# An early one-kilobyte load, the place of its transpose, and new due times in a planned attention and feed-forward kernel

## The chip, the cores and the metric

The kernel runs on one core of a Trainium2 chip. A core has five engines with a queue of instructions each: PE (TensorE, matrix products; its weight loads are listed as PEld), DVE (VectorE), ACT (ScalarE), POOL (GpSimd) and SP (SyncE, which issues most transfers). Sixteen DMA engines move data between the device memory and the core's memory. Engines wait for one another through semaphores. The metric is device microseconds (us) of one execution, the median of several runs; smaller is better.

## The reference

Two blocks read the same x (2048 rows of 512, bf16) and are mixed by a gate per row:

```python
def _A_ref(x, wqkv, wo):                       # H = 32 heads of 16, window W = 256
    q, k, v = qkv[0], qkv[1], qkv[2]           # from x @ wqkv
    scores = jnp.einsum("bhqd,bhkd->bhqk", q, k) * (Dh ** -0.5)
    mask = (idx[:, None] - idx[None, :] >= 0) & (idx[:, None] - idx[None, :] < W)
    scores = jnp.where(mask[None, None], scores, -1e9)
    p = _softmax(scores, axis=-1)
    o = jnp.einsum("bhqk,bhkd->bhqd", p, v)
    return (...)(o, 0, 2, 1, 3).reshape(B, S, D) @ wo

def _B_ref(x, w1, w3, w2):                     # F = 1376
    h = _silu(x @ w1) * (x @ w3)
    return h @ w2

g = _sigmoid((x * gate_w).sum(-1, keepdims=True))
return g * _A_ref(x, A_wqkv, A_wo) + (1 - g) * _B_ref(x, B_w1, B_w3, B_w2)
```

The einsums of the feed-forward block are written here as products.

## The kernel before

**What PE has to do.** The rows are taken in 16 tiles of 128 and 4 quarters of 512 (index `tq` or `tcb`). Attention goes through four columns `c` of 128 features (eight heads each). For a column and a quarter `projections` computes k, q (L374, four matmuls of 512 columns each) and v (L432). For each of the 16 row tiles, `main_batch` computes scores into the tile `su` (L493, eight matmuls), ScalarE takes their exponential into `E` (L498), VectorE masks the diagonal (L479), and `pv` multiplies with v (L588). Every quarter also has a `far_batch` (L525 and, in the last, L533) for the far edge of the window; GpSimd masks that (L552). `pv` divides by the sum and multiplies by the gate on VectorE (L596, L599), and SP transposes the result into `OT` by a DMA (L605).

The feed-forward block works quarter by quarter: 11 blocks `f` of up to 128 features with w1 and w3 (L651, four matmuls of 512 columns for each of the two), tanh on ScalarE (L656), two VectorE operations (L660, L665) into `hT`, and then the product with w2 for four row tiles (L702). `output` multiplies `OT` with wo (L731), adds the feed-forward part (L735) and stores (L740).

The partial results of all these products go through four banks of PSUM, `ch`; the scores have a place of their own, `su`.

**What sets the order.** Nothing is scheduled by the compiler. `opening` (L255) writes its instructions in the order of the code: zeros for `warm`, the identity, 27 matmuls of zeros (`warm_up`, L253), then all the loads. A load on `nc.sync` is issued by SP, one on `nc.scalar` by ScalarE's queue. `load_w` (L245) loads a weight block for a range of features; with `both=True` SP takes its first half and ScalarE's queue the second. In the built program the DMAs take eight semaphores in turn, and a DMA that takes one again waits until the earlier transfer of that semaphore has landed.

All later work is a list of operations in a `Plan`. Each has an engine, an expected duration, what it depends on, the buffers it takes and frees, and a due time. `emit` (L62) walks through an imagined time: of the operations that can start first, it writes the one with the earliest due time. The imagined landing times of the loads are the table `landed`. So due times and `landed` set the order in which instructions stand in each engine's queue; the hardware then works through each queue in that order. The due times come from four numbers: attention is spread evenly over `TA` from `T0` (`at(c, t)`), the feed-forward block from `TF0` to `TF1` (`ffn_due`). Projections are due a `lead` before the scores they serve, P·V and the outputs some us after `at`.

**The opening.** x's first quarter is loaded plainly and turned on PE (L312, 16 transposes of 128 columns), then evacuated (L317 on VectorE, L319 on ScalarE). Then come eight more zeros (`warm_up(8)`, L328). The first feed-forward block f = 0 is cut in halves of 256 columns, so that it can begin when half of the quarter is there. gate_w, 512 numbers, is loaded as four rows of 128 (`gwr`) and turned on PE by a tiny transpose (`gw_turn`, L334); VectorE copies the result next to the first 128 columns of wv (L338, L342), so that the v projection of column 0 gives the gate's sum as a 129th column. In the program before, PE's instructions stand thus: 27 zeros, 16 transposes of x, 8 zeros, w1 for the first half, the turn of gate_w, w3 for the first half, w1 for the second half, k, q, w3 for the second half, w1 of f = 1, v, the first scores, w3 of f = 1.

Of the kernel before, what the change touches and what calls it, by code (L numbers as in the profile page):

```python
# [15 lines left out]
P = 128  # L16
# [22 lines left out]
class Plan:  # L39
# [6 lines left out]
    def add(self, eng, dur, fn, deps=(), due=0.0, take=(), free=(), lat=None):  # L46
        if lat is None:
            lat = 0.2 if eng == "PE" else 0.08
        op = Op(eng, dur, fn, deps, due, list(take), list(free), lat, len(self.ops))
        self.ops.append(op)  # L50
        return op
# [73 lines left out]
def kernel(  # L125
# [20 lines left out]
    NDC = D // P  # L146
# [21 lines left out]
    w3_sb = pp.tile([P, NDC, F], BF16, name="w3_sb")  # L168
# [24 lines left out]
    ch = [ps.tile([P, 512], F32, name=f"ch_{i}") for i in range(4)]  # L193
# [3 lines left out]
    add = plan.add  # L197
# [47 lines left out]
    def load_w(dst, src, f0, f1, both=False):  # L245

        rows = src[:, f0:f1].rearrange("(c p) f -> p c f", p=P)
        for eng, c0, c1 in ((nc.sync, 0, 2), (nc.scalar, 2, 4)) if both else ((nc.sync, 0, 4),):
            eng.dma_start(out=dst[:, c0:c1, f0:f1], in_=rows[:, c0:c1, :])

    def warm_up(n):
        for i in range(n):
            nc.tensor.matmul(su[:, 0, 0:P], lhsT=warm[:], rhs=warm[:], start=True, stop=True)  # L253

    def opening():  # L255
        nc.vector.memset(warm[:], 0.0)
        constants()
        warm_up(WARM)

        nc.scalar.activation(out=gt[:, 0:4], in_=warm[:, 0:4], func=ACT.Tanh)  # L260
        load_x(0, 2, nc.sync)
        load_x(2, 4, nc.scalar)
        load_w(w1_sb, B_w1, 0, 2 * P, True)
        load_w(w3_sb, B_w3, 0, 2 * P, True)
        nc.scalar.dma_start(out=gwr[:], in_=gate_w.rearrange("(c p) -> c p", p=P))
        for b in (1, 0, 2):
            load_w(wqkv_sb, A_wqkv, b * D, b * D + 2 * P)
        for f0, f1, tq in ((2 * P, 6 * P, 1), (6 * P, F, 2)):
            load_w(w1_sb, B_w1, f0, f1)
            load_w(w3_sb, B_w3, f0, f1)  # L270
            turn_x(tq)
        nc.sync.dma_start(out=w2_sb[:, 0:NFC - 1, :],
                          in_=B_w2[0:(NFC - 1) * P, :].rearrange("(f p) n -> p f n", p=P))
        nc.sync.dma_start(out=w2_sb[0:FL, NFC - 1, :], in_=B_w2[(NFC - 1) * P:F, :])
        turn_x(3)
        nc.sync.dma_start(out=wo_sb[:], in_=A_wo.rearrange("(c p) n -> p c n", p=P))
        for b in (1, 0, 2):
            load_w(wqkv_sb, A_wqkv, b * D + 2 * P, (b + 1) * D)
        constants2()
        constants3()  # L280
        constants4()
        constants5()


    T0, TA, TF0, TF1 = 10.0, 234.0, 4.0, 246.0
    step = TA / (NDC * NT)
    landed = {"x": [4.0, 4.1, 15.6, 22.0, 30.0], "w13": [4.9, 5.6, 12.6, 19.8], "w2": 28.5,
              "qkv": [6.6, 7.4, 8.2, 34.0], "wo": 31.5, "gw": 5.8}

    def at(c, t):  # L290
        return T0 + step * (c * NT + t)
# [4 lines left out]
    x_in = [arrive(u) for u in landed["x"]]  # L296
    w13_in = [arrive(u) for u in landed["w13"]]
    qkv_in = [arrive(u) for u in landed["qkv"]]
    gw_in = arrive(landed["gw"])
# [4 lines left out]
    for m in range(4):  # L304
# [16 lines left out]
        a = add("PE", 0.25, tr, [x_in[m // 2]], 0.1 * m, take=[(job, "ch")])  # L321
# [3 lines left out]
    for tq in range(1, NTC):  # L325
        xt_ready[tq].append(x_in[tq + 1])

    add("PE", 0.44, lambda: warm_up(8), [x_in[1]], 0.5)  # L328


    gjob = Job()
# [9 lines left out]
    def wv0_copy():  # L341
        nc.vector.tensor_copy(out=wv0[:, :, 0:P], in_=wqkv_sb[:, :, 2 * D:2 * D + P])  # L342

    a = add("PE", 0.1, gw_turn, [gw_in], 7.0, take=[(gjob, "ch")])
    wv0_ready = [add("DVE", 0.15, gw_out, [a], 9.0, free=[(gjob, "ch")]),
                 add("DVE", 0.3, wv0_copy, [qkv_in[2]], 9.0)]
    gate_ready = []
# [7 lines left out]
    ejob = {}  # L355

    def projections(c, tq):
        lead = 14.0 if c else 3.0
        due = at(c, 4 * tq) - lead
        war = []  # L360
        if c:
# [18 lines left out]
        a = plan.pieces(HALF, 0.2172, lambda lo, hi: chain(kj, D, lo, hi), src[:-1] + [qkv_in[0 if c < 2 else 3]], due, [(kj, "ch")])  # L380
# [23 lines left out]
            k_ready[(c, tq)] = [m0, m1]  # L404

        qj = Job()
        qdue = due if tq == 0 else at(c, 4 * tq - 4) - lead + 4.0

        qeng = "ACT" if (c, tq) == (0, 0) else "DVE"

# [3 lines left out]
        a = plan.pieces(HALF, 0.2172, lambda lo, hi: chain(qj, 0, lo, hi), src[:-1] + [qkv_in[1 if c < 2 else 3]] + qwar, qdue, [(qj, "ch")])  # L414
# [6 lines left out]
        for m0, nm in ([(4 * tq, 2), (4 * tq + 2, 2)] if c == 0 else [(4 * tq, 4)]):  # L421
# [26 lines left out]
            if c == 0:  # L448
                a = plan.pieces((0, 1, 2), 0.225, vmm, src + vwar + wv0_ready, vdue, [(vj, "ch")])
            else:  # L450
                a = plan.pieces(HALF, 0.225, vmm, src + vwar, vdue, [(vj, "ch")])
# [115 lines left out]
        return res, last_mask  # L567

    def pv(c, i, main, far):
        due = at(c, i) + 2.0  # L570
        job = Job()
        blocks = []
        for back in (2, 1, 0):
            if i - back >= 0:
                blocks.append((i - back, 0, P * back))
                blocks.append((i - back, 1, 320 + P * back))
        deps = [main[t] for t, par, off in blocks if par == 0]
        if i >= 2:
            deps.append(far[i - 2])
        for tq in sorted({t // 4 for t, par, off in blocks}):  # L580
            deps += v_ready[(c, tq)]

        def mm(lo, hi):
            po = ch[job.at["ch"]]
            for s in range(lo, hi):
                for bi, (t, par, off) in enumerate(blocks):
                    e = E[ejob[(c, t // 4)].at["E"]][:, t % 4, s].rearrange("p a q -> p (a q)")
                    nc.tensor.matmul(po[:, 34 * s:34 * s + 34], lhsT=e[:, off:off + P],  # L588
                                     rhs=vbd[:, 2 * t + par, s, :], start=(bi == 0),
                                     stop=(bi == len(blocks) - 1))  # L590

        def po8(job):
            return ch[job.at["ch"]][:, 0:8 * (DH + 1)].rearrange("p (h d) -> p h d", d=DH + 1)

        def rec():
            nc.vector.reciprocal(out=rden[job.at["oc"]][:], in_=po8(job)[:, :, DH:DH + 1])  # L596

        def norm():
            nc.vector.scalar_tensor_tensor(out=oc[job.at["oc"]][:], in0=po8(job)[:, :, 0:DH],  # L599
                                           scalar=gq[:, i:i + 1],  # L600
                                           in1=rden[job.at["oc"]][:].to_broadcast([P, 8, DH]),
                                           op0=ALU.mult, op1=ALU.mult)

        def tr():
            nc.sync.dma_start_transpose(out=OT[:, c, i * P:(i + 1) * P],  # L605
                                        in_=oc[job.at["oc"]][:].rearrange("p h d -> p (h d)"))

        frees = [(ejob[(c, h)], "E") for h in range(max(0, i - 2) // 4, i // 4 + 1)]
        a = plan.pieces(HALF, 0.026 * len(blocks), mm, deps, due, [(job, "ch")], free=frees)
        pv_ops[(c, i)] = a  # L610
        b = add("DVE", 0.21, rec, [a], due, take=[(job, "oc")])
        d = add("DVE", 0.35, norm, [b, gate_ready[i // 4]], due, free=[(job, "ch")])
        ot_ready[(c, i)] = add("SP", 1.1, tr, [d], due, free=[(job, "oc")], lat=1.3)
# [25 lines left out]
    for tcb in range(NTC):  # L639
        hj = Job()  # L640
        hs = []
        for f in range(NFC):
            fs = fsz(f)
            due = ffn_due(1.73)
# [24 lines left out]
            if tcb == 0 and f == 0:  # L669

                def half_first(j, w, k, half=half):
                    return lambda: half(j, w, 0, NDC, t0=256 * k, t1=256 * (k + 1))

                a = add("PE", 0.436, half_first(job, w1_sb, 0), xt_ready[0][0:2] + [w13_in[0]], due,
                        take=[(job, "ch")])
                b = add("PE", 0.436, half_first(up, w3_sb, 0), [a, w13_in[1]], due, take=[(up, "ch")])
                a = add("PE", 0.436, half_first(job, w1_sb, 1), xt_ready[0][2:4] + [a], due)
# [15 lines left out]
        for mm in range(4):  # L693
            m = 4 * tcb + mm
            due = ffn_due(2.38)
# [25 lines left out]


    def output(m, n0, n1, queue):
        due = at(NDC - 1, m) + 6.0
        job = Job()
        part = n1 - n0

        def omm(lo, hi):
            pso = ch[job.at["ch"]]
            for c in range(lo, hi):  # L730
                nc.tensor.matmul(pso[:, 0:part], lhsT=OT[:, c, m * P:(m + 1) * P], rhs=wo_sb[:, c, n0:n1],  # L731
                                 start=(c == 0), stop=(c == NDC - 1))

        def oev():
            nc.vector.tensor_tensor(out=ot[job.at["ot"]][:, 0:part], in0=ch[job.at["ch"]][:, 0:part],  # L735
                                    in1=bsb[:, m, n0:n1], op=ALU.add)

        def odma():
            eng = nc.sync if queue == "SP" else nc.scalar
            eng.dma_start(out=out2d[m * P:(m + 1) * P, n0:n1], in_=ot[job.at["ot"]][:, 0:part])  # L740

        a = plan.pieces(HALF, 0.2172 * part / 512, omm, [ot_ready[(c, m)] for c in range(NDC)] + [wo_in], due,
                        [(job, "ch")])
        b = add("DVE", 0.69 * part / 512 + 0.02, oev, [a, b_ready[m]], due, take=[(job, "ot")],
                free=[(job, "ch")])
        add(queue, 0.55, odma, [b], due, free=[(job, "ot")], lat=1.3)
# [39 lines left out]
```

## Time and profile before

| | |
|---|---|
| runs of the kernel | 256.56 us median (254.38, 256.56, 256.69) |
| profiled execution | 257.61 us |
| its span (first to last instruction) | 255.8 us |
| PE busy | 248.4 us |
| VectorE, ScalarE, GpSimd busy | 184.4, 183.2, 107.8 us |
| PE matmuls of w1 and w3 (L651) | 360, 89.9 us |
| scores' exponentials (L498) | 60, 1876 ns each |
| mean granted clock of PE | 0.993 |

The span begins with the first instruction that the profiler recorded and ends with the last; the time has some 1.8 us around it. Busy time of a group is the time in which at least one of its instructions was under way; matmuls overlap, so their mean duration is longer than the distance at which they follow one another. A digit of the clock's line is the clock that PE was granted, in tenths of full speed.

### The profile page before, as it was taken

Reading aid. Unit: us, or ns where it says so; the run is one execution under the profiler, and the core shown is the slowest. Engines: PE = TensorE matmul, PEld = TensorE weight load, DVE = VectorE, ACT = ScalarE, POOL = GpSimd, SP = SyncE. Lnnn points to the kernel's source line nnn. Section 1 sums busy time; section 2 is a strip of 40 time slices with the busy share of each in tenths; the row PEclk is TensorE's granted clock in tenths of the full one; section 3 lists DMA queues with packets and bytes.
Section 4 is the critical chain, followed back from the end, with each engine's and each line's share of the span. In section 5 each row is a group of like instructions: output and inputs, shape, how many; then the busy total and the mean of one; then the engine's idle time right before and its main releaser. Section 6 shows DMA issues by size and latency. Waiting matters only on the chain.

```text
span 255.8 us, 8017 instructions
## 1 busy us (share of the span) xinstructions
PE 248.4 (97%) x3440; PEld 135.2 (53%) x3440; DVE 184.4 (72%) x402; ACT 183.2 (72%) x181; POOL 107.8 (42%) x97
## 2 busy tenths in 40 slices
PE   8699999999999999999999999999999999999995
PEld 8354555655464555555464555555554545545462
DVE  5168789867478888776478878867578787787562
ACT  3077889888677888867678797976588677685521
POOL 7000946070346364592357464473165460290300
PEclk9799999999999999999999999999999999999999
DMA  7999920000000000000000000000010111111112
GB/s 205 303 256 246 274 64 10 14 8 13 10 8 18 13 12 8 14 14 13 5 13 13 11 12 14 14 5 18 3 23 26 33 49 32 52 30 51 49 33 67
DMA packets 28107, 13.14 MB, mean 51 GB/s; under 512 B 17352, under 2 KB 28072, under 8 KB 28072
## 3 DMA queue, kind: packets, MB, share of 16 engines
q1 hardware_dynamic: 27104, 12.04, 19.4%
q10 hardware_dynamic: 968, 0.59, 0.7%
q8 instruction: 27, 0.44, 0.7%
q14 instruction: 8, 0.07, 0.1%
HBM read 6.85 MB, written 2.10 MB: 35 GB/s over the span
## 4 chain that ended last, share of the span: by engine, by line
PE 91%; DMA 5%; ACT 1%; DVE 1%; issue 0%; SPq 0%; DVEq 0%
PE ch L651 30%; PE ch L702 15%; PE ch L588 14%; PE ch L374 11%; PE su L493 8%; PE ch L432 6%; PE ch L731 5%; PE su L525 2%; DMA OT<-oc 2%; DMA gwr<-in_gate_w_dram 2%; ACT E L498 1%; DMA w_sb<-in_B_w_dram 1%; DVE ot L735 0%; DVE vbd L442 0%; PE su L533 0%
## 5 line engine op out<-in xcount | busy, mean ns | idle before, releaser
L498 ACT ACTIVATE E<-su 128x2048 bf16<-128x2048 f32 x60 | 112.6, 1876 | 33.1 <-PE su L493 32.5
L552 POOL TENSOR_SCALAR_AFFINE_SELECT E<-E 64x1024 bf16<-64x1024 bf16 x56 | 65.5, 1169 | 80.1 <-ACT E L540 77.7
L651 PE MATMUL ch<-xT,w_sb 128*128 128x512 bf16 (+2 forms) x360 | 89.9, 378 | 0.0
L398 POOL TENSOR_SCALAR kbd<-kt,rowsA 128x512 bf16<-128x512 bf16 x24 | 37.5, 1572 | 51.9 <-DVE kt L395 34.3
L588 PEld LDWEIGHTS <-E 128*128 128x128 bf16 x1440 | 43.7, 96 | 12.5 <-issue 2.7
L651 PEld LDWEIGHTS <-w_sb 128*128 128x128 bf16 (+1 forms) x360 | 31.6, 100 | 30.9 <-issue 4.6
L588 PE MATMUL ch<-vbd,E 128*128 128x34 bf16 x1440 | 46.3, 177 | 0.1
L702 PE MATMUL ch<-w_sb,hT 128*128 128x512 bf16 (+1 forms) x176 | 43.7, 380 | 0.0
L479 DVE TENSOR_TENSOR E<-E,mdiag 128x512 bf16<-128x512 bf16 x64 | 34.1, 533 | 12.7 <-ACT E L498 11.8
L660 DVE SCALAR_TENSOR_TENSOR h<-tt,ch 128x512 bf16<-128x512 bf16 (+1 forms) x44 | 30.1, 684 | 8.5 <-ACT tt L656 7.9
L374 PE MATMUL ch<-xT,wqkv_sb 128*128 128x512 bf16 x128 | 35.3, 388 | 0.0
L540 ACT ACTIVATE E<-su 128x2048 bf16<-128x2048 f32 (+1 forms) x16 | 26.6, 1663 | 12.2 <-PE su L525 7.2
L656 ACT ACTIVATE tt<-ch 128x512 bf16<-128x512 f32 (+1 forms) x44 | 26.1, 594 | 10.2 <-PE ch L651 9.8
L665 DVE SCALAR_TENSOR_TENSOR hT<-h,ch 128x512 bf16<-128x512 bf16 (+1 forms) x44 | 30.2, 686 | 4.2 <-PE ch L651 0.4
L702 PEld LDWEIGHTS <-hT 128*128 128x128 bf16 (+1 forms) x176 | 15.2, 97 | 17.1 <-issue 2.1
L599 DVE SCALAR_TENSOR_TENSOR oc<-ch,gq,rden 128x128 bf16<-128x128 f32 x64 | 22.5, 351 | 2.3
L493 PE MATMUL su<-qT,kbd 32*128 32x256 bf16 x480 | 23.8, 273 | 0.0
L596 DVE RECIPROCAL rden<-ch 128x8 f32<-128x8 f32 x64 | 13.1, 204 | 12.8 <-PE ch L588 12.5
L493 PEld LDWEIGHTS <-kbd 32*128 32x128 bf16 x480 | 7.1, 92 | 23.4 <-issue 22.9
L707 DVE TENSOR_SCALAR bsb<-ch,omg 128x512 bf16<-128x512 f32 x15 | 11.2, 749 | 10.6 <-PE ch L702 10.4
L374 PEld LDWEIGHTS <-wqkv_sb 128*128 128x128 bf16 x128 | 11.1, 100 | 11.9 <-issue 3.0
L731 PE MATMUL ch<-wo_sb,OT 128*128 128x512 bf16 (+1 forms) x68 | 16.6, 366 | 0.6 <-DMA OT<-oc 0.6
(54 smaller groups left out, 146.5 us busy)
## 6 DMA issues: line engine op xcount, KB each, us to landing
out_dram<-ot SPq DMA_DIRECT2D x15, 128.0 KB, 1.8
wqkv_sb<-in_A_wqkv_dram SPq DMA_DIRECT2D x6, 256.0 KB, 5.5
w_sb<-in_B_w_dram SPq DMA_DIRECT2D x1, 1280.0 KB, 7.0
w_sb<-in_B_w_dram SPq DMA_DIRECT2D x2, 608.0 KB, 4.5
w_sb<-in_B_w_dram SPq DMA_DIRECT2D x2, 512.0 KB, 4.8
OT<-oc SPq DMA_TRANSPOSE x64, 2.2
wo_sb<-in_A_wo_dram SPq DMA_DIRECT2D x1, 512.0 KB, 5.0
xs<-in_A_x_dram SPq DMA_DIRECT2D x1, 256.0 KB, 2.9
```

What stands on the lines that cost most here:

```text
L374: nc.tensor.matmul(pst[:], lhsT=wqkv_sb[:, dc, col + c * P:col + (c + 1) * P], rhs=xT[:, dc, tq * 512:(tq + 1) * 512], start=(dc == 0), st ...
L398: nc.gpsimd.tensor_scalar_mul(out=kv[:, :, h, :], in0=kt[kj.at["kt"]][:].rearrange("p (k t) -> p k t", t=KB), scalar1=rowsA[:, h:h + 1])
L479: nc.vector.tensor_tensor(out=e, in0=e, in1=mdiag[:, None, :].to_broadcast([P, 8, KB]), op=ALU.min)
L493: nc.tensor.matmul(su[:, s, par * 256:(par + 1) * 256], lhsT=kbd[r, 2 * t + par, :, :].rearrange("p a k -> p (a k)"), rhs=qT[r, q0:q0 + 25 ...
L498: nc.scalar.activation(out=E[ej.at["E"]][:, t % 4, :, :, 0:256], in_=su[:].rearrange("p s (a q) -> p s a q", a=2), func=ACT.Exp, scale=SCALE)
L552: nc.gpsimd.affine_select(out=e[lo:lo + KB], in_=e[lo:lo + KB], pattern=[[0, 16], [-1, KB]], compare_op=ALU.is_ge, fill=0.0, base=-1, chan ...
L588: nc.tensor.matmul(po[:, 34 * s:34 * s + 34], lhsT=e[:, off:off + P], rhs=vbd[:, 2 * t + par, s, :], start=(bi == 0), stop=(bi == len(bloc ...
L651: nc.tensor.matmul(ch[job.at["ch"]][0:fs, t0:t1], lhsT=w[:, dc, f * P:f * P + fs], rhs=xT[:, dc, tcb * 512 + t0:tcb * 512 + t1], start=(dc ...
L660: nc.vector.scalar_tensor_tensor(out=h1[job.at["h1"]][0:fs, :], in0=tt[job.at["tt"]][0:fs, :], scalar=1.0, in1=ch[job.at["ch"]][0:fs, :], ...
L665: nc.vector.scalar_tensor_tensor(out=hT[0:fs, f, :], in0=h1[job.at["h1"]][0:fs, :], scalar=0.5, in1=ch[up.at["ch"]][0:fs, :], op0=ALU.mult ...
L702: nc.tensor.matmul(bps[:], lhsT=hT[0:fs, f, mm * P:(mm + 1) * P], rhs=w2_sb[0:fs, f, :], start=(f == 0), stop=(f == NFC - 1))
L731: nc.tensor.matmul(pso[:, 0:part], lhsT=OT[:, c, m * P:(m + 1) * P], rhs=wo_sb[:, c, n0:n1], start=(c == 0), stop=(c == NDC - 1))
```

## The change

The diff does five things. In `opening`, the load of gate_w is issued on ScalarE's queue right behind that queue's half of w1, ahead of w3; and w3's first block is loaded by SP alone. `landed` is given other numbers for x, w1, w3. Two zeros stand behind the transposes of x and not eight. The turn of gate_w is due at 7.7 and not 7.0. And the due times are others: attention over 224 us and not 234, the feed-forward block from 0 to 240 and not from 4 to 246, projections of later columns 18 us ahead and not 14 (q behind the first quarter then stands 16 ahead of its point, and not 10), P·V 1 us before its point and not 2 behind, outputs 8 us behind and not 6.

```diff
@@ opening
         load_w(w1_sb, B_w1, 0, 2 * P, True)
-        load_w(w3_sb, B_w3, 0, 2 * P, True)
         nc.scalar.dma_start(out=gwr[:], in_=gate_w.rearrange("(c p) -> c p", p=P))
+        load_w(w3_sb, B_w3, 0, 2 * P)
@@
-    T0, TA, TF0, TF1 = 10.0, 234.0, 4.0, 246.0
+    T0, TA, TF0, TF1 = 10.0, 224.0, 0.0, 240.0
     step = TA / (NDC * NT)
-    landed = {"x": [4.0, 4.1, 15.6, 22.0, 30.0], "w13": [4.9, 5.6, 12.6, 19.8], "w2": 28.5,
+    landed = {"x": [4.0, 4.4, 15.6, 22.0, 30.0], "w13": [5.3, 5.8, 12.6, 19.8], "w2": 28.5,
@@
-    add("PE", 0.44, lambda: warm_up(8), [x_in[1]], 0.5)
+    add("PE", 0.11, lambda: warm_up(2), [x_in[1]], 0.5)
@@
-    a = add("PE", 0.1, gw_turn, [gw_in], 7.0, take=[(gjob, "ch")])
+    a = add("PE", 0.1, gw_turn, [gw_in], 7.7, take=[(gjob, "ch")])
@@ projections
-        lead = 14.0 if c else 3.0
+        lead = 18.0 if c else 3.0
@@
-        qdue = due if tq == 0 else at(c, 4 * tq - 4) - lead + 4.0
+        qdue = due if tq == 0 else at(c, 4 * tq - 4) - lead + 2.0
@@ pv
-        due = at(c, i) + 2.0
+        due = at(c, i) + -1.0
@@ output
-        due = at(NDC - 1, m) + 6.0
+        due = at(NDC - 1, m) + 8.0
```

In the built program PE's instructions in the opening then stand thus: 27 zeros, 16 transposes of x, 2 zeros, w1 and w3 for the first half, w1 and w3 for the second half, k, q, w1 and w3 of f = 1, the turn of gate_w, the first scores, two matmuls of k of column 1, half of v, two more of k of column 1, the other half of v, w1 and w3 of f = 2. From there on nearly every engine's order differs in places; the amount of work is the same.

## Prediction

> **What bounds the kernel now.** I read the page first: busy shares, then the 40 slices.
>
> ```profile
> PE 248.4 (97%) x3440; PEld 135.2 (53%) x3440; DVE 184.4 (72%) x402; ACT 183.2 (72%) x181; POOL 107.8 (42%) x97
> ...
> PE   8699999999999999999999999999999999999995
> ...
> PEclk9799999999999999999999999999999999999999
> ```
>
> PE is busy for 248.4 of 255.8 us, and the only dents are in the first two slices and the last. The second slice also has the low clock digit. So PE's own work sets the time, and what can be had lies in the opening. Second view, PE's timeline there (start, length, instruction; the bracket is idle time before it and what ended it):
>
> ```profile
> 5.60 0.93 PE L253 MATMUL su<-warm 128*128 128x128 bf16 x8
> 6.37 0.60 PE L651 MATMUL ch<-xT,w_sb 128*128 128x256 bf16 x4
> 9.49 0.17 PE L334 MATMUL ch<-ident,gwr 4*128 4x4 bf16 x1 [2.52 <-DMA gwr<-in_gate_w_dram]
> 9.60 1.85 PE L651 MATMUL ch<-xT,w_sb 128*128 128x256 bf16 x8
> 11.24 2.81 PE L374 MATMUL ch<-xT,wqkv_sb 128*128 128x512 bf16 x8
> ```
>
> Eight zeros, four w1 matmuls, then PE stands before the tiny transpose of gate_w (L334) until that 1 KB has landed. The eight wqkv matmuls then take 2.81 us, 0.35 each, where later ones start every 0.216 us. The table of stretches says why (the third column is PE busy; PEclk, the granted clock, is third from the end):
>
> ```profile
> 6.30:9.60 3.30, 0.78 (x10) 0.46 (x7) 0.00 (x0) 0.00 (x0) 0.00 (x0) 1.00 1.13 309
> 9.70:13.00 3.30, 3.30 (x13) 1.73 (x13) 0.87 (x2) 0.60 (x1) 0.00 (x0) 0.50 1.23 288
> 13.10:16.50 3.40, 3.40 (x37) 2.10 (x35) 2.13 (x4) 2.28 (x6) 0.00 (x0) 1.00 0.80 206
> ```
>
> The stretch with the stall is followed by one at half the clock. Third view, ScalarE's queue: gate_w is issued at 4.95, long after the rows before it (1.49 plus 1.01).
>
> ```profile
> 1.49 1.01 ACTq L249 DMA_DIRECT2D w_sb<-in_B_w_dram  x2
> 4.95 0.52 ACTq L265 DMA_DIRECT2D gwr<-in_gate_w_dram  x1
> ```
>
> In the built program this issue waits on a DMA semaphore that SP's half of w1 used first (that landed 1.30 + 3.62 = 4.92); there are eight such semaphores, dealt out in turn. Last, the waits: after the opening PE waits visibly once, for a transposed tile.
>
> ```profile
> PE ch L334 <- DMA gwr<-in_gate_w_dram: 2.5, 1, 2.5
> ...
> PE ch L731 <- DMA OT<-oc: 0.6, 1, 0.6
> ```
>
> **The change, part by part.** *gate_w third on ScalarE's queue, its turn later.* The issue moves to about 2.0 us and in the built program waits for nothing (its semaphore is fresh). The turn now stands behind both feed-forward blocks of f = 0 and 1, k and q. PE's idle time goes: the last w1 matmul starts at 6.70 and needs 0.11, the turn starts at 9.49, so **2.7 us**. The turn's own 0.11 us stays. Its copy on DVE (L338, 0.18 us) must end before the v projection; between lie the first scores and two k matmuls, 0.33 + 0.43 us, so it costs nothing, and some 0.2 us without that cover.
>
> *The clock.* With no stall, no empty stretch, no half clock. At half clock 7 matmuls of 256 columns started 0.213 us apart and not 0.109 (0.73 us), and four and a bit of 512 columns 0.427 and not 0.216 (0.91): **1.65 us**.
>
> *Two zeros for eight.* Six of 0.107 us go: **0.64 us**. What they hid: the evacuations for w1's first half (L317, 4.57 plus 0.85 = 5.42) and ScalarE's half of w1 (1.49 + 3.9 = 5.4). PE now reaches w1 at 5.81, so both are just in time. But the clock is granted at 6.26 (the zeros before it start every 0.107 us, 128 columns at half rate), so two of the four w1 matmuls run at half: **minus 0.2 us**.
>
> *w3 whole on SP.* Before, w3 landed in halves at 6.4 (1.80 + 4.6, SP) and 6.9 (2.0 + 4.8, ScalarE). Now 256 KB in one transfer, behind xs and half of w1. PE wants it at 5.81 + 0.43 + 0.22 = 6.46. Not before 6.36, when SP's half alone landed. Not after 7.6, when SP's fourth transfer landed (wk, 2.31 + 5.3): up to it SP moved 768 KB, up to w3's end it now moves 640. I take 6.6, between the halves, since the sum of bytes up to there is unchanged: **minus 0.2 us** (0 to 1.1). Behind this waiting weight load stands everything on PE.
>
> The Trainium skill (DMA: Bandwidth & Descriptors, "Queues, rings and completion order") says that each DMA engine takes turns between the queues that have work, packet by packet. By it ScalarE's queue runs empty and SP's then has the whole rate: 128 KB more behind SP's half, at the 309 GB/s of the second stretch, land 0.42 us after 6.36, at 6.8, and the term is 0.4; if SP kept half the rate it would be 7.2 and 0.8. Both are estimates inside the bounds.
>
> *SP's later issues.* w1's second block now waits on w1's first half (4.93) and not on w3 (6.36): issued some 1.4 us earlier. The transposes of x behind it come about 0.6 us earlier, since w3's second block waits for w3 as before. PE comes to the second blocks at 13.9 by my sum (12 matmuls of f = 0 to 8.0, k and q to 9.7, f = 1 to 11.5, turn and scores to 12.1, k of column 1 and v to 13.9); they landed at 10.7 and 12.2 before (6.38 + 4.3, 6.79 + 5.4). It wants x's second quarter at 16.9; that was in at 14.6 (11.53 + 3.1). Covered, with 1.7 and 2.3 us.
>
> *ScalarE early.* The first exp (1.88 us) now stands ahead of the evacuation of v: 12.1 to 14.0, then two groups of 0.7 us to 15.4, tanh to 16.0. The bank of the first v group is free when DVE has copied, at 15.3, and f = 3 wants it at 16.0. Covered by 0.7 us.
>
> *The due times* (attention's and feed-forward's ends, leads, P·V and outputs) only reorder. I summed PE's row durations along both programs. Between one score batch and the next lie 2.57 us in the median in both (least 2.21 before, 2.18 after; exp takes 1.88). From a batch to its P·V at least 2.54 before, 2.91 after (exp and mask: 1.88 + 0.43). From P·V to its output product at least 3.55 before, 3.36 after (0.20 + 0.35 on DVE, 2.2 for the transposed tile). The last 5 us hold the same instructions in the same order. I cost it at 0; it could save the one visible wait or add such waits.
>
> **The sum:** 2.7 + 1.65 + 0.64 − 0.2 − 0.2 = 4.6; my walk by positions gives 4.4 (PE had done the same work at 17.83 + 0.43 = 18.26, now at 13.9). I take 4.5. The profiled execution took 257.61 us (span 255.8): it becomes 253.1, span 251.3. The median of the runs, 256.56, lies 1.05 lower; so the forecast is **252.1 us**.
>
> **The rivals.** *The clock.* The row: 0.78 us of work in 3.3 was followed by half clock, a full stretch by full clock. Between, nothing is shown. If fewer zeros and the wait for w3 leave a stretch too thin, one more runs at half: 3.4 us that do the work of 1.7, so **253.8**. For it: only 0.2 to 1.1 us of waiting separate the rows' two cases. Against: 0.2 in 3.4 is little beside 2.5. The Trainium skill (TensorE: Matmul & The Clock Gate, Part 1) ties the gate to a free-running window of about 3.4 us, full clock after a busy one, half after an idle one. The rows agree on the length, not on "idle": here 24% busy was too little. By the rule the six zeros could be what fills the first window, and 253.8 would be the time.
>
> *w3 late.* At 7.6, wk and wq behind it: 1.0 more, **253.1**, and with the clock's fall 254.8.
>
> *The data bound.* PE runs 4.5 us ahead of loads that come hardly earlier. If x or second blocks slip past the 1.7 and 2.3 us, PE waits there: 2 us back, **254.1**. Against: SP issues them earlier.
>
> *Slower: transposes behind stores.* Outputs and P·V transposes share SP's queue. At 199.47 a transpose met a store (200.75) and took 4.5 us to land in place of 2.2; PE lost 0.76 us at its output product (0.6 by the waits). If new dues put stores beside transposes, each of 16 outputs can cost that. Six eat the gain, ten make it 0.76 × 10 − 4.5 = 3.1 slower, **259.7**. For it: the shortest cover falls to 3.36, and the order on SP changes in two places. Against: just two.
>
> *It doesn't do what it says:* gate_w lands late although third, PE waits at the later turn. It would take until after 11.5 us: excluded but for a hundredth.
>
> **How the numbers follow.** Forecast 0.66, clock 0.13, w3 late 0.10, data bound 0.05, slower 0.05, no effect 0.01. Low end: the whole 5.0 us of the three gains and the one visible wait, 0.76: 256.56 − 5.75 = 250.8. High end: the clock and w3 late together, 254.8, rounded to 255.0. About 1% (2.6 us, so 254.0 and 259.1) is what a measurement of this kernel can tell from none; the runs before spread over 2.3. Faster by over 1%: nearly all of the forecast, half of the clock's case, most of w3's, half of data's: 0.79. Same 0.16, slower 0.05.
>
> **What would show it.** PE's timeline without an idle bracket over 0.5 us after 6 us; the wqkv matmuls 0.22 apart; PEclk near 1.00 from 6.3 on; the first 512-column block of f = 2 near 14 us; then every slice at 9 and the same last 5 us. The forecast is wrong if PEclk shows 0.50 past 6.3, if an idle bracket names w_sb or xT between 6 and 20 us, or if L731 waits for OT more than twice.

## The result

The changed kernel takes **251.87 us** in the median of six runs (251.53 to 252.67); beside it the kernel before took 256.62 (254.38 to 258.98). Two of the six runs of the kernel before (258.46 and 258.98) are of a slower state that this program sometimes falls into, and the ratio of the means without them is 0.985, 95% interval 0.981 to 0.989. The forecast was 252.1 us, range 250.8 to 255.0. The profiled execution took 251.68 us, span 249.9 us: 5.9 us less than that of before, where the prediction said 4.5. That is one execution; the medians lie 4.75 us apart.

The page of the changed kernel, PE's busy time and its line and the clock's in the 40 slices:

```profile
PE 244.9 (98%) x3434; PEld 132.9 (53%) x3434; DVE 184.1 (74%) x402; ACT 184.0 (74%) x181; POOL 107.4 (43%) x97
...
PE   7999999999999999999999999999999999999994
...
PEclk9999999999999999999999999999999999999999
```

The dent and the low clock of the second slice are gone, and PE was busy 3.5 us less (244.9 against 248.4). PE's timeline in the opening (start, length, instruction, idle before it and what ended that):

```profile
4.83 0.28 PE L253 MATMUL su<-warm 128*128 128x128 bf16 x2
5.14 0.60 PE L651 MATMUL ch<-xT,w_sb 128*128 128x256 bf16 x4
6.12 1.48 PE L651 MATMUL ch<-xT,w_sb 128*128 128x256 bf16 x12 [0.38 <-DMA w_sb<-in_B_w_dram]
7.44 1.89 PE L374 MATMUL ch<-xT,wqkv_sb 128*128 128x512 bf16 x8
9.16 1.89 PE L651 MATMUL ch<-xT,w_sb 128*128 128x512 bf16 x8
10.99 0.17 PE L334 MATMUL ch<-ident,gwr 4*128 4x4 bf16 x1
...
13.13 1.89 PE L651 MATMUL ch<-xT,w_sb 128*128 128x512 bf16 x8
```

The turn of gate_w (L334) has no bracket any more; the only one in the opening is 0.38 us before w3. The eight wqkv matmuls take 1.89 us, not 2.81. f = 2 begins at 13.13, where the same work was done at 18.26 before. The same stretches as before (third column PE busy, PEclk third from the end):

```profile
6.30:9.60 3.30, 3.30 (x23) 1.99 (x22) 1.66 (x3) 0.83 (x2) 0.00 (x0) 1.00 1.14 320
9.70:13.00 3.30, 3.30 (x34) 1.72 (x32) 2.06 (x6) 2.96 (x4) 0.00 (x0) 1.00 1.21 295
```

PE is busy throughout both, at full clock. So 5.1 of the 5.9 us are gained ahead of f = 2; where the last 0.8 come from was not traced.

### The profile page after: what moved, and what is told of

The parts are those of the page before. It is cut to its first block, busy times and chain, and to the rows that moved or that the text cites. A ratio compares the mean times of both kernels' runs of the same rounds, so it can differ in the third digit from the quotient of the medians.

```text
span 249.9 us, 8005 instructions
## 1 busy us (share of the span) xinstructions
PE 244.9 (98%) x3434; PEld 132.9 (53%) x3434; DVE 184.1 (74%) x402; ACT 184.0 (74%) x181; POOL 107.4 (43%) x97
## 4 chain that ended last, share of the span: by engine, by line
PE 93%; DMA 4%; DVE 1%; SPq 1%; issue 0%
PE ch L651 31%; PE ch L702 15%; PE ch L588 15%; PE ch L374 12%; PE su L493 8%; PE ch L432 6%; PE ch L731 5%; DMA OT<-oc 2%; PE su L525 2%; DMA w_sb<-in_B_w_dram 2%; DVE ot L735 1%; SPq L605 0%; DVE h L660 0%; SPq L249 0%; PE su L533 0%
## 5 line engine op out<-in xcount | busy, mean ns | idle before, releaser
L651 PEld LDWEIGHTS <-w_sb 128*128 128x128 bf16 (+1 forms) x360 | 30.9, 99 | 31.0 <-issue 4.6
L374 PE MATMUL ch<-xT,wqkv_sb 128*128 128x512 bf16 x128 | 34.1, 379 | 0.0
L432 PEld LDWEIGHTS <-xT 128*128 128x128 bf16 x256 | 15.6, 97 | 4.6 <-issue 1.3
```

What stands on the lines that cost most here:

```text
L374: nc.tensor.matmul(pst[:], lhsT=wqkv_sb[:, dc, col + c * P:col + (c + 1) * P], rhs=xT[:, dc, tq * 512:(tq + 1) * 512], start=(dc == 0), st ...
L432: nc.tensor.matmul(pst[:, mm * w:(mm + 1) * w], lhsT=xT[:, dc, m * P:(m + 1) * P], rhs=rhs, start=(dc == 0), stop=(dc == NDC - 1))
L651: nc.tensor.matmul(ch[job.at["ch"]][0:fs, t0:t1], lhsT=w[:, dc, f * P:f * P + fs], rhs=xT[:, dc, tcb * 512 + t0:tcb * 512 + t1], start=(dc ...
```

## The experiments

Each kernel was timed beside runs of the kernel before on the same chip. In the diffs the minus lines are those of the kernel that is named as its base.

### The early loads alone

Base: the kernel before. PE's order is untouched.

```diff
-        load_w(w3_sb, B_w3, 0, 2 * P, True)
         nc.scalar.dma_start(out=gwr[:], in_=gate_w.rearrange("(c p) -> c p", p=P))
+        load_w(w3_sb, B_w3, 0, 2 * P)
```

> The kernel before with the new loads alone: gate_w third on ScalarE's queue, w3 whole on SP. PE's order is that of before, with eight zeros and the turn of gate_w behind the first four w1 matmuls. The theory of the prediction: gate_w lands before 6.8 us, so the wait of 2.7 us and the half clock behind it (1.65) go, while the zeros (0.64) stay and hide w3: 256.6 - 4.35 = 252.3 us, idle before the turn under 0.2. Rival, that the new order carries the gain: only the wait of 2.7 goes at most and is partly taken back by the next load, 254 to 255.

Measured: 252.38 us (252.23 to 253.15); before 256.86. ScalarE's queue and PE in its profile:

```profile
1.99 0.62 ACTq L264 DMA_DIRECT2D gwr<-in_gate_w_dram  x1
```

```profile
5.30 0.66 PE L651 MATMUL ch<-xT,w_sb 128*128 128x256 bf16 x4
6.21 0.17 PE L334 MATMUL ch<-ident,gwr 4*128 4x4 bf16 x1 [0.26 <-DMA gwr<-in_gate_w_dram]
6.43 1.05 PE L651 MATMUL ch<-xT,w_sb 128*128 128x256 bf16 x8
```

The issue moved from 4.95 to 1.99 us. PE waits 0.26 us at the turn, a little more than the 0.2 expected, though the turn stands where it stood. The new loads alone give 4.5 us, and 252.38 is within a tenth of the theory's 252.3.

### The later turn with the old loads

Base: the changed kernel, with the loads of before. The turn is late, and the due times, the landing table and the two zeros are the new ones too.

```diff
-        nc.scalar.dma_start(out=gwr[:], in_=gate_w.rearrange("(c p) -> c p", p=P))
-        load_w(w3_sb, B_w3, 0, 2 * P)
+        load_w(w3_sb, B_w3, 0, 2 * P, True)
+        nc.scalar.dma_start(out=gwr[:], in_=gate_w.rearrange("(c p) -> c p", p=P))
```

> The changed kernel with the loads of before: w3 in halves on two queues, gate_w behind them and issued near 4.9 us. PE's order is that of the changed kernel. The theory: gate_w lands near 9.4 and the turn stands near 11, so nothing waits for it; w3's second half lands near 6.8, 0.2 to 0.7 later than in the changed kernel: 252.1 to 252.6 us. So the late turn alone takes the gain, as the early issue alone does. Rival, that the early issue is needed: PE idles at the turn and the time is above 254.

Measured: 251.97 us (251.82 to 253.34), as the changed kernel and just under the range expected. gate_w is issued at 4.75 us, late as before, and the turn has no bracket:

```profile
11.42 0.17 PE L334 MATMUL ch<-ident,gwr 4*128 4x4 bf16 x1
```

Either way takes the whole gain: gate_w may come early, or be wanted late. The run also says that w3 in halves on both queues costs nothing as long as gate_w is issued after it.

### w3 in halves, gate_w third

Base: the changed kernel.

```diff
-        load_w(w3_sb, B_w3, 0, 2 * P)
+        load_w(w3_sb, B_w3, 0, 2 * P, True)
```

> The changed kernel with w3's first block in halves on two queues again; gate_w stays third on ScalarE's queue. In the built program the fourth DMA of that queue now takes a semaphore again and waits for SP's half of w1 (4.8 us). Theory of the eight semaphores: that half of w3 is issued near 4.8 and lands near 9, PE waits 2.5 us at w3's first matmul, and the clock falls behind it: 251.9 + 2.7 + 1.65 = 256.2, at least 254.6. Rival (queues matter, not semaphores; one queue or two is the same): 251.9 within 0.3.

Measured: 255.69 us (253.85 to 256.70) beside 252.11 for the changed kernel, timed with it. ScalarE's queue, then PE:

```profile
4.84 0.39 ACTq L249 DMA_DIRECT2D w_sb<-in_B_w_dram  x1
```

```profile
5.82 1.22 PE L651 MATMUL ch<-xT,w_sb 128*128 128x256 bf16 x6
9.31 1.65 PE L651 MATMUL ch<-xT,w_sb 128*128 128x256 bf16 x10 [2.27 <-DMA w_sb<-in_B_w_dram]
11.18 2.34 PE L374 MATMUL ch<-xT,wqkv_sb 128*128 128x512 bf16 x5 [0.22 <-issue]
```

The wait has moved from gate_w to w3: the fourth DMA of ScalarE's queue is issued at 4.84, as gate_w was before (4.95). In the built programs gate_w's load there and w3's second half here wait for the same semaphore, that of SP's half of w1; in the changed kernel none of ScalarE's three early loads waits for one. So w3 lies whole on SP not for the queues' sake; it takes one transfer out of the count of eight. The runs of this kernel fall into two groups by granted clock: five at 1.00 with a median of 254.04 us, seven at 0.993 with 256.33. The theory's 256.2 is met by the seven; the five waited and kept the clock, which it did not foresee.

### PE kept busy during the wait

Base: the kernel before. Nothing is taken away; zeros stand in the wait.

```diff
     def gw_turn():
-        nc.tensor.transpose(...)
+        warm_up(40); nc.tensor.transpose(...)
```

> The kernel before with 40 matmuls of zeros on PE ahead of the turn of gate_w (2.2 us at 0.056 each), so that PE is busy while it waits for gate_w; the turn itself cannot come earlier. It measures the clock by itself. The theory (idle time takes the clock): no stretch at half clock after the turn, wqkv matmuls 0.216 apart, 256.6 - 1.65 = 255.0 us. Rival (the half clock has another cause): a stretch at 0.50 as before, 256.6 us or more.

Measured: 254.87 us (254.58 to 255.02, ten runs) beside 256.86 for the kernel before; ratio 0.9925, 95% interval 0.9898 to 0.9952. PE and the stretches:

```profile
5.98 2.40 PE L253 MATMUL su<-warm 128*128 128x128 bf16 x40
9.41 0.17 PE L334 MATMUL ch<-ident,gwr 4*128 4x4 bf16 x1 [1.03 <-DMA gwr<-in_gate_w_dram]
...
10.62 1.67 PE L374 MATMUL ch<-xT,wqkv_sb 128*128 128x512 bf16 x7
```

```profile
6.30:9.60 3.30, 2.27 (x40) 2.08 (x38) 0.00 (x0) 0.00 (x0) 0.00 (x0) 1.00 1.14 321
9.70:13.00 3.30, 3.25 (x22) 1.99 (x22) 1.87 (x5) 1.27 (x3) 0.00 (x0) 1.00 1.37 202
```

The turn comes as late as before (9.41), yet the kernel is 2.0 us faster, for useless work. That is the price of the half clock, measured apart from the wait. What then still separates it from the early loads alone, timed beside it at 252.38, is 2.5 us: the wait. The rival, another cause of the half clock, is out: no stretch here shows 0.50.

### Old due times

Base: the changed kernel.

```diff
-    T0, TA, TF0, TF1 = 10.0, 224.0, 0.0, 240.0
+    T0, TA, TF0, TF1 = 10.0, 234.0, 4.0, 246.0
```

The leads, P·V's and the outputs' due times are the old ones too.

> The changed kernel with the old due times (attention over 234 us, feed-forward from 4 to 246, leads, P.V and outputs as before); loads, landing table, two zeros and the later turn are new. The theory prices the due times at 0: 252.1 us, within 0.5 of the changed kernel, no idle time over 0.5 us from 7 us on. Rival, that the due times carry part of the gain: 253.5 or more, with idle brackets on PE in the middle or at the end.

Measured: 253.29 us (253.09 to 253.63): outside the theory's 0.5 and just short of the rival's 253.5. Two places of its profile show where some of it goes, both in front of P·V (PE lines; the bracket is idle time):

```profile
24.73 0.60 PE L651 MATMUL ch<-xT,w_sb 128*128 128x512 bf16 x2
25.63 0.76 PE L588 MATMUL ch<-vbd,E 128*128 128x34 bf16 x24 [0.30 <-DVE qT L413]
...
147.35 0.60 PE L651 MATMUL ch<-xT,w_sb 128*128 128x512 bf16 x2
148.30 0.76 PE L588 MATMUL ch<-vbd,E 128*128 128x34 bf16 x24 [0.34 <-DVE h L660]
```

The brackets count from the end of the row ahead, in which the last matmul is shown longer than its distance. Counted by distances (two matmuls of 0.216 us from 24.73 and from 147.35) PE stood there for 0.47 and 0.52 us. By the releasers, this order has P·V reach for a bank that VectorE has not yet emptied. That is about 1.0 of the 1.4 us; the rest stays open.

But is it the due times, or this one order? Another kernel tells: the kernel before with the new loads and two zeros, which has old due times and PE's old order.

```diff
-    add("PE", 0.44, lambda: warm_up(8), [x_in[1]], 0.5)
+    add("PE", 0.44, lambda: warm_up(2), [x_in[1]], 0.5)
```

> The kernel before with the new loads and two zeros: PE's order is that of before, old due times included. It tells whether the old due times as such cost something, or only the order that the planner made of them in the run with old due times (253.3 us). Theory that due times cost nothing: as the run with the new loads alone (252.4) or up to 0.3 less, since two zeros or eight made no difference. Rival, that old due times cost 1.4: 253.3.

Measured: 252.54 us (252.43 to 253.04) beside 252.31 (251.97 to 253.49) for the changed kernel, timed with it. In its profile PE waits for nothing after the first zeros. So old due times as such cost 0.2 us, which is inside the spread of the runs, and not 1.4. The planner's order changes nearly everywhere when the landing table and the turn's due time change, and one such order is 0.7 us worse than another with the same due times (253.29 and 252.54, timed on two chips).

### New due times alone

Base: the kernel before.

```diff
-    T0, TA, TF0, TF1 = 10.0, 234.0, 4.0, 246.0
+    T0, TA, TF0, TF1 = 10.0, 224.0, 0.0, 240.0
-        lead = 14.0 if c else 3.0
+        lead = 18.0 if c else 3.0
...
```

The due times of q, P·V and the outputs are the new ones too.

> The kernel before with the new due times alone; loads, eight zeros, landing table and the turn's due time are old. The planner now puts the turn of gate_w behind all of f = 0 (twelve matmuls more ahead of it). gate_w lands near 9.4 as before; PE has work to about 8.2 and waits some 1.2 us. Theory: 251.9 + 1.2 = 253.1, with the granted clock at 1.00 or only partly lower, since the empty stretch is half as long. Rival, that the new due times carry the gain: 252 or less. Rival, that they are worth nothing here: 256 or more.

Measured: 253.61 us (253.14 to 254.70), granted clock 0.998 to 1.00, beside 257.00 for the kernel before. PE:

```profile
6.85 1.71 PE L651 MATMUL ch<-xT,w_sb 128*128 128x256 bf16 x12 [0.50 <-DMA w_sb<-in_B_w_dram]
9.71 0.17 PE L334 MATMUL ch<-ident,gwr 4*128 4x4 bf16 x1 [1.16 <-DMA gwr<-in_gate_w_dram]
9.82 1.90 PE L374 MATMUL ch<-xT,wqkv_sb 128*128 128x512 bf16 x8
```

The due times help by moving the turn, without being meant to: it lands behind twelve more matmuls, the wait shrinks from 2.52 to 1.16 us, and the clock holds. Alone they are thus worth 3.4 us, nearly all of it in the opening: about 1.0 of waiting, by the brackets, and the 2.0 of the clock. That it is 0.5 more than the theory's 253.1 fits the 0.50 us of waiting for w3, which the theory had left out.

### Zeros: two, eight, none

Base: the changed kernel, `warm_up(8)` and `warm_up(0)` in place of `warm_up(2)`; the changed kernel itself as a mark.

> The changed kernel with eight zeros behind the transposes in place of two. The prediction's sum: six more zeros cost 0.64 us and hide its 0.2 of waiting for w3: about 0.4 more, 252.3. Other theory, from the changed kernel's profile (PE idles 0.38 us before w3, and some 0.5 us lie between the starts): the zeros only fill that wait, so 0.0 to 0.2 more, 251.9 to 252.1.

> The changed kernel with no zeros behind the transposes. If w3's landing sets the start, the same time as with two, 251.9, with a longer idle bracket before w3's first matmul. If the zeros are what keeps the clock's first window full, some runs come 1 to 1.7 us later, at a lower granted clock. If only zeros were in the way, 0.2 less.

> The changed kernel itself, as the mark for the three kernels beside it: 251.9 us.

Measured: eight 251.93 us (251.40 to 252.72), none 251.89 (251.23 to 252.42), the mark 252.11 (251.83 to 252.97). No difference. In the mark's profile PE idles before w3:

```profile
5.32 0.60 PE L651 MATMUL ch<-xT,w_sb 128*128 128x256 bf16 x4
6.72 1.48 PE L651 MATMUL ch<-xT,w_sb 128*128 128x256 bf16 x12 [0.80 <-DMA w_sb<-in_B_w_dram]
```

With eight zeros the same 16 matmuls run without a bracket, from 6.46, and so they do with none, from 5.60:

```profile
5.61 1.04 PE L253 MATMUL su<-warm 128*128 128x128 bf16 x8
6.46 1.94 PE L651 MATMUL ch<-xT,w_sb 128*128 128x256 bf16 x16
...
5.60 2.61 PE L651 MATMUL ch<-xT,w_sb 128*128 128x256 bf16 x16
```

So the bracket does not hang on the zeros alone. In these two profiles the 16 transposes ahead took 1.91 us, in the mark's 1.25: there the clock rose earlier, and PE came to w3 before it had landed. The medians agree with the expectation that the zeros only fill a wait; the profiles, one for each, do not show it apart from the clock. And the clock did not need the zeros: without any, all six runs have a mean granted clock of 0.998 or 1.00.

### w1's second half ahead of w3

Base: the changed kernel. The two operations between w1's first half and w3's second half trade places; no other instruction moves.

```diff
-                b = add("PE", 0.436, half_first(up, w3_sb, 0), [a, w13_in[1]], due, take=[(up, "ch")])
-                a = add("PE", 0.436, half_first(job, w1_sb, 1), xt_ready[0][2:4] + [a], due)
+                b = add("PE", 0.436, half_first(job, w1_sb, 1), [a, w13_in[1]], due, take=[(up, "ch")])
+                a = add("PE", 0.436, half_first(up, w3_sb, 0), xt_ready[0][2:4] + [a], due)
```

> The changed kernel with one swap on PE: w1's second half (four matmuls of 256 columns, 0.44 us) stands ahead of w3's first half, so that PE has work while w3 lands; nothing else moves. PE idled 0.38 and 0.80 us there in two profiles of the changed kernel. Theory: 0.3 to 0.5 less than the mark beside it, 251.5. Rival (PE then waits for the evacuations of x, which end near 5.8): no gain.

> The changed kernel itself, as the mark for the three kernels beside it: 252.0 us.

Measured: 252.28 us (251.06 to 253.00) beside 252.31 for the mark (251.97 to 253.49). Inconclusive: the 0.3 to 0.5 us do not show in the medians. The bracket before w3 is gone from its profile and that execution took 251.06, the least of all; but other runs of it took 252.7 and 253.0, and the profile is of one run. The mark's own profile shows how far w3's landing alone can move:

```profile
7.39 1.49 PE L651 MATMUL ch<-xT,w_sb 128*128 128x256 bf16 x12 [1.59 <-DMA w_sb<-in_B_w_dram]
```

That execution took 253.49 us.

## Why the prediction was right

The direction, the mechanism and the size were as forecast; the two large terms carry it, and of the small ones two errors cancelled. By its steps:

- **gate_w's wait, 2.7 us.** Right. Three kernels that reach it in different ways (early issue, later turn, both) end between 251.9 and 252.4, and with the clock held it measures 2.5. The cause of the late issue was argued from the semaphores' turns; the halves of w3 show it, since there w3's second half takes that semaphore again and it, not gate_w, is issued near 4.8.
- **The clock, 1.65 us.** Right in kind, somewhat small. The zeros in the wait give 2.0. The kernel before gives a second reading, from its 41 runs beside the experiments: six with a granted clock of 0.999 or 1.00 took 254.3 to 255.0, 27 at 0.992 or 0.993 took 255.9 to 257.9, medians 254.8 and 257.0; the 254.8 is what the kernel with zeros in the wait takes (254.87). Eight at 0.987 took 257.7 to 259.3. By the means, one stretch of 3.4 us at half clock (1.7 of 255.8 us) makes 0.993 and two would make 0.987; that is an estimate, no profile shows such a run. The halves of w3 give 2.3. One stretch explains 1.7 of the 2.0 to 2.3; what the other 0.3 to 0.6 are was not tried, nor why the same wait takes the clock in most runs and not in all.
- **Two zeros for eight, 0.64 us, w1's first matmuls at half clock, −0.2, and w3's landing, −0.2.** The sizes were off. Together they were to give 0.24; zero, two and eight zeros differ by 0.2 at most, with no order. The worst of them is PE's wait for w3. By the prediction's own times it is 0.14 us (6.6 less 6.46; its two other estimates of 0.4 and 0.8 are 0.34 and 0.74), and the profiles of the changed kernel show 0.38, 0.80 and 1.59. It was missed from both sides. w3 was taken to land at 6.6 and not before 6.36; in nine profiles with w3 whole on SP it landed 4.3 to 5.5 us after its issue at 1.80, at 6.1 to 7.3, and in seven of them by 6.4. PE was taken to want it at 6.46; in the three profiles of the changed kernel it had done w1's first half at 5.74, 5.92 and 5.79, since the clock rose before the zeros there (the transposes took 1.10, 1.25 and 1.19 us, against 1.91 before). All later work stands behind w3, so PE won nothing by being early: w3's matmuls began at 6.12, 6.72 and 7.39, around the 6.6 of the sum. That the errors cancel is luck. In the profile of the result PE reached f = 2 at 13.13, 0.77 ahead of the walk by positions: 0.56 of it by w3's landing at 6.1 (k begins at 7.44 and not 8.0), and 0.26 at the turn and the first scores (0.34 us for 0.6).
- **The due times, 0.** Right beside the other edits: 0.2 us, inside the spread, between the changed kernel and the old order with new loads. Wrong if taken as their own worth, for alone they give 3.4 us by moving the turn; the gains of the parts overlap (4.5 for the loads, 3.4 for the due times, some 4.7 for all) and can't be added. Nor do distances along PE's order tell of every order: the run with old due times has two waits of half a us, and a median and a least distance say little of the one place where a bank is late.
- **Later loads and ScalarE's early queue, 0.** Right: no bracket of the changed kernel's profile names them.
- **The rivals.** "The clock" did not come: no run of the changed kernel has a mean below 0.997. "w3 late" came in part: in one execution w3 kept PE for 1.59 us, beyond the bound of 1.1, and that execution was 1.2 us above the median of the six timed together. "Slower" did not; PE waited for transposed tiles for 0.6 us in the changed kernel's profile and 1.1 in the third, against 0.6 before.
- **Its signs.** The wqkv matmuls 0.22 apart and the clock at 1.00 from 6.3 on came. No idle bracket over 0.5 us after 6 us held in the profile of the result (0.38) and not in the two others (0.80 and 1.59). And one of its signs of being wrong stood in all three: a bracket that names w_sb between 6 and 20 us, at 6.12, 6.72 and 7.39. The sign was too strict, since the sum itself had PE wait for w3 until 6.6; beside it the time held.

On the clock's rule, which the prediction weighed: the Trainium skill (TensorE: Matmul & The Clock Gate, Part 1) says that the window runs freely. These runs agree: PE's first matmul stands at 1.04 us in each profile, and yet the rate doubles at different places, so that the eight zeros take 0.93 us (before), 0.61 (early loads alone) and 1.04 (changed kernel with eight): they start 0.107 us apart at half clock and 0.056 at full. Its rule that half clock follows an idle window does not fit as it stands: a stretch with 0.78 of 3.30 us busy was followed by half clock, one with 2.27 was not. (The stretches are cut at the same times in each run; where the clock's own windows begin, these rows don't show.) The fear drawn from the rule, that six zeros fewer would lose the first window, did not come true: in the profile without zeros w1's matmuls begin at 5.60, and PE is busy for all 3.40 us from 2.80 to 6.20.

## What to carry to other kernels

An issue that starts long after the one before it on its queue waits for something, and where DMA semaphores are dealt out in turn the culprit is a transfer that has nothing to do with it: count the early transfers, and merge or reorder them so that the small one that is needed soon gets a fresh semaphore. A wait of PE can cost more than its length when the clock falls behind it, here 2.0 us on top of 2.5 in most runs, while waits of 1.2 and 1.6 us cost no clock here; useless matmuls in the wait win that part back, and so show how much it is. Edits that remove the same wait overlap: measure each alone and all together before you add them up. Where a planner makes the order, time its new order as a whole: here two orders with the same due times differed by 0.7 us.

## What the runs showed that was not expected

The spread of the kernel before goes with the clock: 254.3 to 259.3 us, in three groups by granted clock. The changed kernel, in which PE does not wait for gate_w, spreads over 2.0 us in 18 runs (251.5 to 253.5) at a granted clock of 0.997 to 1.00; one cause is in sight, the landing of w3, which held PE 0.38 us in one profile and 1.59 us in another with the same instructions.
